# Planning the order of an attention and two-MLP kernel with a shared SBUF port, and folding in pairs

## The chip, the cores and the metric

The kernel runs on one core of a Trainium2 chip. The core's engines run side by side, each through its own list of instructions in order: TensorE (matmul, PE in the rows), VectorE (DVE), ScalarE (ACT), GpSimd (POOL), and SyncE (SP), which here issues most DMAs. An instruction that needs another engine's result waits on a semaphore, and everything behind it on its own engine waits too. SBUF is the on-chip memory, PSUM the matmul's accumulators (eight banks, `bank` in the rows). The metric is the device time of one execution in microseconds; the median of three runs of the kernel before is 742.17 us (740.36 to 742.63).

## The reference

```python
a = softmax(phi)                      # over the sequence, axis 2
k_m, v_m = a^T k, a^T v               # 32 memory rows for each of 4 x 8 heads
attn = softmax(q k_m^T / 8) v_m       # 4 x 8 heads, 576 tokens, 64 wide
x = attn, heads beside each other     # 2304 tokens x 512
x = ((x w_a) * (x w_b)) w_out         # 512 -> 1536 -> 512
h = x w_in                            # 512 -> 2048
out = (h * sigmoid(1.702 h)) w_out2   # 2048 -> 512
```

All in float32. The kernel splits each float32 operand into a high and a low part (fp32r) and multiplies in three passes, high x high, low x high, high x low.

## The kernel before, in words

**Stages on TensorE.** (1) Attention, to about 119 us, by eight steps `n` (batch `b`, half of the heads `g`): `memory(n)` transposes phi (L554 to L580), makes the memory keys and values (L596, L618) and the scores (L635), and `softmax` makes the attention weights `attn`, split in high and low. (2) The values are never multiplied with the weights: `fold(g, b)` (L798) multiplies the values of batch `b` into group `g` of w_a and w_b, 24 folds of 16 small fp32 matmuls, each followed by `fold_out`: a ScalarE copy (L818) and a VectorE subtraction (L820) for each of two banks, which make the high and low part of the folded weights `eff`. `gated` (L852) multiplies attn with a folded weight, 48 matmuls for a fold in two halves `u` (24 each), and multiplies the two products (L876). (3) `project` (L1014, to 373 us) is w_out by Strassen's seven products. (4) `step` and `quad` (L1290, to 547) are w_in, by seven products again, with the additions on VectorE (L1332, one input in PSUM) and the gate on ScalarE. (5) `proj2` (L1499) and `proj2_seven` (L1530) are w_out2.

**Combines.** Each split into high and low (`hi_lo`) is a ScalarE copy (L349) and a subtraction; Strassen's sums of weights and tokens are additions and subtractions of SBUF tiles; the softmax has two more. All go through `combine` (L343), which lets the planner choose GpSimd or VectorE. `sum_tokens` (L896) is always GpSimd's. `decode_piece` (L445, L449, L451) turns pieces of weights that come as 64-bit words into float32; L451 is VectorE's.

**What sets the order.** No list is written by hand. `Order` holds a clock for each engine and a set of streams (generators) with priorities. Each stream asks for an engine, with the time from which it can start and a duration; the planner starts the request that can start first (in steps of 40 ns), then by priority, and moves the engine's clock on. For a choice of engines (`_plan`) it takes the one that would end first, with a handicap in ns for VectorE (`W0` until the last stage, then `W1`). DMA landings are reckoned from a rate and a delay (`RATE0` in the first stage). The instructions come out in the order in which the planner starts them, and the chip keeps that order on each engine. The planner's numbers never reach the chip. While the first weights are not there, `warm_up` puts fill matmuls (L1605) on TensorE, as many as the planner's time asks for.

**Durations before.** `dve`, `act` and `pool` reckon fixed costs plus a rate; the class `Lengths` holds them and is switched between stages by `measured()`, `crowded()`, `calm` and `short()`. Where GpSimd or VectorE may combine, the durations are multiplied by `Lengths.pool` and `Lengths.both`.

Of the kernel before, what the change touches and what calls it, by code (L numbers as in the profile page):

```python
# [20 lines left out]
HOP, HOP_PE = 130.0, 200.0  # L21
W0 = 300.0
W1 = 0.0
# [12 lines left out]
PT1 = 15  # L36
FRONT = 1.0, 1.0, 1.0
RATE0 = 300.0, 2500.0
RATE = 330.0, 3000.0
# [6 lines left out]
PY = 5  # L46
RX = 12
BETWEEN = (0, 2, 4, 3, 3, 2, 2, 0)

# [6 lines left out]

class Lengths:
    dve, act, psum = 68, 94, 52
    six, wide, three = 740, 2.54, 650
    pool, both, slow = 1.0, 1.0, 1.0  # L60


def measured():
    Lengths.dve, Lengths.act, Lengths.psum = 150, 205, 160
    Lengths.six, Lengths.wide, Lengths.three = 795, 2.71, 690
    Lengths.pool, Lengths.both, Lengths.slow = 1.15, 1.4, 1.15


def crowded():
    measured()  # L70
    Lengths.pool, Lengths.both, Lengths.slow = 1.3, 1.75, 1.55


def short():
    Lengths.dve, Lengths.act, Lengths.psum = 68, 94, 52
    Lengths.pool, Lengths.both, Lengths.slow = 1.0, 1.0, 1.0


def dve(n, fast=False):
    return Lengths.dve + n / (1.92 if fast else 0.96)  # L80


def act(n, psum=False):
    return (Lengths.psum if psum else Lengths.act) + n / 1.2


def pool(n):
    return 150 + 2.1 * n
# [18 lines left out]
class Order:  # L107
# [9 lines left out]
    def __init__(self):  # L117
        self.clock = {PE: 0.0, ACT: 0.0, DVE: 0.0, POOL: 0.0}
        self.dma, self.marks, self.streams, self.count = 2000.0, {}, [], 0

        self.handicap = {DVE: W0}
        self.rate, self.land = RATE0

# [41 lines left out]
    def _plan(self, s):  # L165

        r = s[3]
        if not isinstance(r[0], dict):
            t = max(self.clock[r[0]], r[1] + (70.0 if r[0] == PE else 0.0))
            return (t if len(r) < 4 else max(t, min(x[1] for x in r[3].free))), r[0], r[2]  # L170
        best = None
        for e, d in r[0].items():
            t = max(self.clock[e], r[1])
            before = sum(
                x[3][2] for x in self.streams if x is not s and x[3][0] == e and x[:2] < s[:2] and x[3][1] <= t + d
            )
            if best is None or t + before + d + self.handicap.get(e, 0.0) < best[0]:
                best = t + before + d + self.handicap.get(e, 0.0), (t, e, d)
        return best[1]

    def run(self):
        while self.streams:
            if self._settle():
                continue
            plans = []
            for s in self.streams:
                r = s[3]
                if (isinstance(r[0], dict) or r[0] in self.clock) and (len(r) < 4 or r[3].free):
                    plans.append((self._plan(s), s))
            (t, e, d), s = min(plans, key=lambda x: (x[0][0] // 40, x[1][0], x[1][1]))  # L190
            self.clock[e] = t + d
            r = s[3]
            what = e if isinstance(r[0], dict) else r[3].take() if len(r) > 3 else None
            self._resume(s, (t + d + (HOP_PE if e == PE else HOP), what))
# [3 lines left out]
def tile_mem_attention_moe_moe2(  # L198
# [140 lines left out]
    def combine(t, dst, in0, in1, op, n):  # L339

        both = {POOL: Lengths.pool * pool(n), DVE: Lengths.both * dve(n)}
        t, e = yield {DVE: dve(n)} if alone[0] else both, t
        (nc.gpsimd if e == POOL else nc.vector).tensor_tensor(out=dst, in0=in0, in1=in1, op=op)  # L343
        return t
# [91 lines left out]
    def decode_piece(t, i, name, part, n, m):  # L436
# [5 lines left out]

        slow = Lengths.slow
        t, _ = yield ACT, t, act(512)
# [4 lines left out]
        nc.scalar.activation(out=lw, in_=top, func=AF.Copy, scale=2.0 ** -5, bias=2.0 ** -6 - 0.5)  # L449
        t, _ = yield DVE, t, slow * dve(512)  # L450
        nc.vector.scalar_tensor_tensor(  # L451
# [78 lines left out]
    def memory(n):  # L530
# [8 lines left out]
        if n >= NHG:  # L539

            t, e = yield {POOL: 900, ACT: act(HG * C0 * M)}, max(t, et[1])
            src = ph[0].rearrange("p h c m -> p c h m")
            dst = et[0].rearrange("p c s x -> p c (s x)").rearrange("p c (h m) -> p c h m", h=HG)
            if e == POOL:
                nc.gpsimd.tensor_copy(dst, src)
            else:
                nc.scalar.activation(out=dst, in_=src, func=AF.Copy)
        part = 240 if n < NHG else 70
        t, ba = yield PE, t, part * last, bank_a
# [23 lines left out]

        t, _ = yield PE, t, 70 * last
# [4 lines left out]
        t1, _ = yield PE, t2, 70  # L579
        nc.tensor.transpose(bb[0][:, P:2 * P], et[0][:, last].rearrange("p s x -> p (s x)"), ident)  # L580
# [140 lines left out]
    def close_attention():  # L721
# [15 lines left out]
        pa.release()  # L737
        measured()
        nonlocal py, pw
# [87 lines left out]
    def gated(g, b, u):  # L827
# [10 lines left out]
        for j, i in ((0, 0), (1, 0), (0, 1), (1, 1)) if wide else ((0, 0), (0, 1), (1, 0), (1, 1)):  # L838
            if True:
                if not wide:  # L840
                    t, ps = yield PE, t0, Lengths.six, bank_m
                    dst = ps[0]
                elif j == 0:
                    t, ps = yield PE, t0, Lengths.six, pair_s
                    dst = ps[0][:, j]
                else:
                    t, _ = yield PE, t0, Lengths.six
                    dst = ps[0][:, j]
# [43 lines left out]
    def sum_tokens(t, g, b, gr):  # L892
        b11, b21, b12, b22 = (gr[0][:, i] for i in range(4))
        for dst, in0, in1 in ((b11, b12, b11), (b12, b22, b12), (b22, b22, b11), (b21, b21, b22)):
            t, _ = yield POOL, t, Lengths.pool * pool(U)
            nc.gpsimd.tensor_tensor(out=dst, in0=in0, in1=in1, op=ALU.subtract)  # L896
# [8 lines left out]
    def have(*key):  # L905
        return od.marks.get(key)
# [241 lines left out]

    def calm():

        for p in (1, 2):
            for r in range(2):
                yield "mark", "yc", p, r
        measured()

    def room_projected():

        od.spawn(9, calm())
        nonlocal p2
# [16 lines left out]
    def room_last():  # L1176

        short()
        alone[0] = True
# [29 lines left out]
        for p in range(F2 // P // 2):  # L1209
            yield "mark", "wt", p  # L1210
        short()
        give(fw_s, views(acc, 2 * FN, 1))
# [394 lines left out]
    def main():  # L1607
        yield from all_gated()
        od.spawn(9, part_again())
        room_gated()  # L1610
        crowded()
        for p in range(NP):
# [23 lines left out]
    with tc.manual_schedule():  # L1636
# [7 lines left out]
        n0 = 2 * NHG  # L1644
        measured()
        Lengths.pool, Lengths.both, Lengths.slow = FRONT

# [54 lines left out]
```

## Time and profile before

| What | us |
|---|---|
| Median of three runs | 742.17 |
| The profiled execution | 740.76 |
| Its span, first to last instruction | 739.0 |
| TensorE busy | 729.0 (99%) |
| VectorE busy | 535.2 (72%) |
| ScalarE busy | 437.9 (59%) |
| GpSimd busy | 294.1 (40%) |

A busy share is an average over stages. The waits that end the kernel are found where TensorE stops; how full another engine is in that stretch says whether it can be the cause. An instruction's row gives its start and duration; on VectorE and GpSimd the duration holds what it waits for the other's use of SBUF.

### The profile page before, as it was taken

What the parts mean: (1) busy time and instruction counts of PE and PEld (TensorE: products, weight loads), DVE (VectorE), ACT (ScalarE), POOL (GpSimd) and SP (SyncE); (2) the same over time, 40 slices, a digit from 0 to 9 for tenths busy, and PEclk for the clock granted to TensorE, in tenths of its full rate; (3) what the DMA queues carried; (4) which work ended last, traced back from release to release, by engine and by line L of the source; (5) the groups of instructions that cost most, each with busy time, mean ns of one, the idle gap of its engine ahead of it and who ended that gap; (6) DMA issues with size and microseconds to landing.
All of it is one profiled execution on the core that took longest, in us unless ns stands there. A gap on an engine that the chain in (4) does not pass through costs nothing.

```text
span 739.0 us, 14874 instructions
## 1 busy us (share of the span) xinstructions
PE 729.0 (99%) x5480; PEld 687.0 (93%) x5480; DVE 535.2 (72%) x910; ACT 437.9 (59%) x852; POOL 294.1 (40%) x278
## 2 busy tenths in 40 slices
PE   9999999999999999999999999999999999999997
PEld 8877888888889999999999999999998889999997
DVE  3988786568983447945999666676657988888774
ACT  3877664677873447547867676666555564444441
POOL 0414376458896616824998343233250000000000
PEclk9999999999999999999999999999999999999999
DMA  8999854886688875676536888875597474444411
GB/s 269 333 342 298 293 200 153 260 282 218 227 257 281 283 203 165 177 207 190 200 114 203 278 251 267 269 258 186 190 298 244 158 233 137 125 144 144 143 30 29
DMA packets 112600, 157.74 MB, mean 213 GB/s; under 512 B 8592, under 2 KB 89232, under 8 KB 112528
## 3 DMA queue, kind: packets, MB, share of 16 engines
q1 hardware_dynamic: 107168, 147.32, 62.8%
q10 hardware_dynamic: 5360, 9.47, 3.7%
q8 instruction: 43, 0.70, 0.4%
q14 instruction: 29, 0.24, 0.1%
HBM read 104.20 MB, written 52.56 MB: 212 GB/s over the span
## 4 chain that ended last, share of the span: by engine, by line
PE 89%; DVE 4%; DMA 4%; issue 1%; ACT 1%; SPq 0%; POOLq 0%; ACTq 0%; POOL 0%; DVEq 0%
PE bank L1290 22%; PE bank L852 21%; PE bank L1530 19%; PE bank L1014 16%; PE bank L798 3%; DMA raw<-w2d 3%; PE bank L1605 2%; PE bank L596 1%; DMA acc<-g2d 1%; DVE attn L343 1%; PE bank L514 1%; DVE w L343 1%; DVE acc L343 1%; PE bank L635 1%; PE bank L576 0%
## 5 line engine op out<-in xcount | busy, mean ns | idle before, releaser
L852 PEld LDWEIGHTS bank<-attn,eff 128*128 128x128 f32 x1152 | 154.2, 188 | 15.4 <-issue 5.2
L852 PE MATMUL bank<-attn,eff 128*128 128x288 f32 x1152 | 162.8, 298 | 0.0
L349 ACT ACTIVATE w<-acc 128x512 fp32r<-128x512 f32 (+2 forms) x144 | 83.9, 591 | 76.9 <-PE bank L1530 47.8
L1332 DVE TENSOR_TENSOR acc<-bank,acc 128x384 f32<-128x384 f32 x168 | 89.4, 552 | 46.4 <-PE bank L1290 30.9
L343 DVE TENSOR_TENSOR w<-acc,w 128x512 fp32r<-128x512 f32 (+2 forms) x122 | 83.0, 685 | 26.3 <-ACT w L349 26.0
L349 ACT ACTIVATE attn<-acc 128x768 fp32r<-128x768 f32 (+2 forms) x84 | 62.6, 752 | 54.9 <-PE bank L1014 38.9
L1014 PE MATMUL bank<-attn,w 128*128 128x384 f32 x504 | 91.9, 335 | 0.7 <-DVE attn L343 0.7
L343 DVE TENSOR_TENSOR attn<-acc,attn 128x768 fp32r<-128x768 f32 (+2 forms) x61 | 67.1, 1111 | 31.9 <-ACT attn L349 30.7
L1014 PEld LDWEIGHTS bank<-attn,w 128*128 128x128 f32 x504 | 87.6, 188 | 2.0 <-DVE attn L343 1.4
L1342 ACT ACTIVATE acc<-acc 128x384 f32<-128x384 f32 x96 | 48.4, 522 | 26.5 <-DVE acc L1332 25.7
L343 DVE TENSOR_TENSOR acc<-acc 128x512 f32<-128x512 f32 (+2 forms) x90 | 60.8, 686 | 0.8 <-POOL w1b L343 0.5
L1290 PE MATMUL bank<-attn,w 128*128 128x384 f32 x288 | 55.1, 334 | 0.0
L896 POOL TENSOR_TENSOR gr<-gr 128x288 f32<-128x288 f32 x48 | 44.2, 922 | 18.7 <-DMA g1d<-gr 8.2
L343 POOL TENSOR_TENSOR attn<-acc,attn 128x768 fp32r<-128x768 f32 (+1 forms) x22 | 37.7, 1726 | 34.6 <-ACT attn L349 34.6
L343 POOL TENSOR_TENSOR w<-dm,w 128x256 fp32r<-128x256 f32 x35 | 30.8, 894 | 51.2 <-ACT w L349 51.1
L1530 PE MATMUL bank<-attn,w 128*128 128x256 f32 x336 | 50.0, 284 | 1.0 <-ACT w L349 0.7
L1290 PEld LDWEIGHTS bank<-attn,w 128*128 128x128 f32 x288 | 50.4, 188 | 0.0
L1014 PE MATMUL bank<-attn,w1b 128*128 128x384 f32 x252 | 47.6, 336 | 0.2 <-DVE attn L343 0.2
L1290 PE MATMUL bank<-w1b,w 128*128 128x384 f32 x224 | 46.2, 334 | 0.0
L1530 PEld LDWEIGHTS bank<-attn,w 128*128 128x128 f32 x336 | 44.5, 192 | 1.4 <-ACT w L349 1.0
L1014 PEld LDWEIGHTS bank<-attn,w1b 128*128 128x128 f32 x252 | 43.9, 188 | 0.9 <-DVE attn L343 0.5
L1290 PE MATMUL bank<-w 128*128 128x384 f32 x224 | 43.8, 334 | 0.0
(172 smaller groups left out, 1374.7 us busy)
## 6 DMA issues: line engine op xcount, KB each, us to landing
acc<-g1d SPq DMA_DIRECT2D x63, 384.0 KB, 3.7
g2d<-acc SPq DMA_DIRECT2D x96, 192.0 KB, 4.1
acc<-g2d SPq DMA_DIRECT2D x14, 1024.0 KB, 6.4
raw<-in_moe_w_out_dram SPq DMA_DIRECT2D x24, 512.0 KB, 4.9
raw<-in_moe_w_in_dram SPq DMA_DIRECT2D x16, 512.0 KB, 5.1
g1d<-gr SPq DMA_DIRECT2D x12, 576.0 KB, 5.3
g1d<-acc SPq DMA_DIRECT2D x8, 576.0 KB, 4.8
raw<-in_moe_w_a_dram SPq DMA_DIRECT2D x16, 256.0 KB, 4.2
```

The source lines that it names most:

```text
L343: (nc.gpsimd if e == POOL else nc.vector).tensor_tensor(out=dst, in0=in0, in1=in1, op=op)
L349: nc.scalar.activation(out=hi, in_=src, func=AF.Copy)
L514: nc.tensor.transpose(ps[0][:, i * P:(i + 1) * P], qs[0][:, 2 * (c0 + i):2 * (c0 + i) + 2, :].rearrange("p e d -> p (e d)"), ident,)
L798: nc.tensor.matmul(ps[c][0][row(h), :], bdv[b][half, h, :], wt["wab", g, h][0][half, :], start=True, stop=True)
L852: nc.tensor.matmul(dst[:, :U], e[:, c, sw, i * CW + j * P:i * CW + (j + 1) * P], attn(b, mv, c, u * U, U), start=(n == 0), stop=(n == 3 * ...
L896: nc.gpsimd.tensor_tensor(out=dst, in0=in0, in1=in1, op=ALU.subtract)
L1014: nc.tensor.matmul(ps[0][:, :N2], w1_of(a, g, sw)[:, r * P:(r + 1) * P], b[0][:, mv, i], start=(first and q == n == 0), stop=(q == NG1 // ...
L1290: nc.tensor.matmul(ps[0][:, :N2], w[:, sw, r, :], y[mv][r], start=(n == 0), stop=(n == 5))
L1332: nc.vector.tensor_tensor(out=s[0], in0=ps[0][:, :N2], in1=x[0], op=ALU.add)
L1342: nc.scalar.activation(out=c[0], in_=c[0], func=AF.Gelu_apprx_sigmoid)
L1530: nc.tensor.matmul(ps[name][0][:, :NB], x[0][:, sw, c, :], moving(b, h // 2 + c, mv), start=(h == c == n == 0), stop=(h > 0 and c == K4 - ...
L1605: nc.tensor.matmul(ps[0][:, :P], ident, ident, start=True, stop=True)
```

## The change

The planner's durations become one set for all stages: `dve(n)` 72 + n / 0.96, `act(n)` 100 + n / 1.2 (56 from PSUM). `Lengths` and its switches go. A combine's duration and some others are marked `Held`: a `Held` request on VectorE or GpSimd can start only when the previous `Held` one, on either engine, has ended (`self.port`). The handicap of VectorE goes from +300 to -300, so the planner takes VectorE unless GpSimd would end over 300 ns sooner. The reckoned rate of the first DMAs goes from 300 to 335 bytes a ns, their delay from 2500 to 1700. In `all_gated`, once attention is closed (`have("close")`), no fold is made while a folded weight is left, and then two are made one behind the other.

```diff
-W0 = 300.0
+W0 = -300.0
-RATE0 = 300.0, 2500.0
+RATE0 = 335.0, 1700.0
+SIX = 798.0
...
-class Lengths:
-    dve, act, psum = 68, 94, 52
-    six, wide, three = 740, 2.54, 650
-    pool, both, slow = 1.0, 1.0, 1.0
-def measured():
-    Lengths.dve, Lengths.act, Lengths.psum = 150, 205, 160
-    Lengths.six, Lengths.wide, Lengths.three = 795, 2.71, 690
-    Lengths.pool, Lengths.both, Lengths.slow = 1.15, 1.4, 1.15
-def crowded():
-    measured()
-    Lengths.pool, Lengths.both, Lengths.slow = 1.3, 1.75, 1.55
...
+class Held(float):
+    pass
...
-def dve(n, fast=False):
-    return Lengths.dve + n / (1.92 if fast else 0.96)
+def dve(n):
+    return 72 + n / 0.96
 def act(n, psum=False):
-    return (Lengths.psum if psum else Lengths.act) + n / 1.2
+    return (56 if psum else 100) + n / 1.2
...
         r = s[3]
         if not isinstance(r[0], dict):
-            t = max(self.clock[r[0]], r[1] + (70.0 if r[0] == PE else 0.0))
+            t = max(self.clock[r[0]], r[1] + (70.0 if r[0] == PE else 0.0), self.port if isinstance(r[2], Held) else 0.0)
...
         for e, d in r[0].items():
-            t = max(self.clock[e], r[1])
+            t = max(self.clock[e], r[1], self.port if isinstance(d, Held) else 0.0)
...
             self.clock[e] = t + d
+            if isinstance(d, Held):
+                self.port = t + d
...
-        both = {POOL: Lengths.pool * pool(n), DVE: Lengths.both * dve(n)}
+        both = {POOL: Held(pool(n)), DVE: Held(dve(n))}
...
-        t, _ = yield DVE, t, slow * dve(512)
+        t, _ = yield DVE, t, Held(dve(512))
...
-            t, e = yield {POOL: 900, ACT: act(HG * C0 * M)}, max(t, et[1])
+            t, e = yield {POOL: Held(700), ACT: act(HG * C0 * M)}, max(t, et[1])
...
-            t, _ = yield POOL, t, Lengths.pool * pool(U)
+            t, _ = yield POOL, t, Held(pool(U))
...
             if y:
                 folded.remove(y)
                 yield from gated(*y, 0)
-                x = ready_to_fold(True)
-            if x:
-                todo.remove(x)
-                folded.append(x)
-                yield from fold(*x)
+                x = None if have("close") and folded else ready_to_fold(True)
+            for _ in range(2):
+                if x:
+                    todo.remove(x)
+                    folded.append(x)
+                    yield from fold(*x)
+                x = ready_to_fold(True) if x and y and have("close") else None
```

The rest of the diff replaces `Lengths.six` by `SIX` and some reckoned transpose durations (70 by 110), and takes out the calls of the removed functions.

What comes out: TensorE, ScalarE and SyncE do the same work in another order (TensorE with 56 fill matmuls instead of 63). GpSimd has 148 instructions instead of 283, VectorE 1053 instead of 912: 135 combines move, and a few small PSUM copies go from ScalarE to VectorE. Lines of the changed kernel are 15 to 17 lower in these rows: L328 is L343, L435 is L451, L546 to L550 are L562 to L566, L644 to L660 are L660 to L676, L781 is L798, L803 is L820, L835 is L852, L859 is L876.

VectorE in the first attention steps, from the fourth decoded weight piece (L451, L435) to the first eff pair (L820, L803); sT is the score tile, sm and aT are the softmax's. Before:

```order
L451 SCALAR_TENSOR_TENSOR acc<-acc,raw_p_76 128x512
L667 TENSOR_SCALAR sm_116<-sm_116 128x9
L667 TENSOR_SCALAR sm_115<-sm_115 128x9
L660 TENSOR_REDUCE sm_117<-sT_112 128x9
L669 RECIPROCAL sm_116<-sm_116 128x9
L669 RECIPROCAL sm_115<-sm_115 128x9
L343 TENSOR_TENSOR sT_112<-sT_112,sm_116 128x288
L676 STREAM_TRANSPOSE aT<-sT_112 128x288
L820 TENSOR_TENSOR eff<-bank,eff 128x512 x2
```

Now:

```order
L435 SCALAR_TENSOR_TENSOR acc<-acc,raw_p_76 128x512
L651 TENSOR_SCALAR sm_116<-sm_116 128x9
L651 TENSOR_SCALAR sm_115<-sm_115 128x9
L644 TENSOR_REDUCE sm_117<-sT_112 128x9
L653 RECIPROCAL sm_116<-sm_116 128x9
L653 RECIPROCAL sm_115<-sm_115 128x9
L328 TENSOR_TENSOR sT_112<-sT_112,sm_117 128x288
L328 TENSOR_TENSOR sT_112<-sT_112,sm_116 128x288
L328 TENSOR_TENSOR sT_111<-sT_111,sm_115 128x288
L660 STREAM_TRANSPOSE aT<-sT_112 128x288
L803 TENSOR_TENSOR eff<-bank,eff 128x512 x2
```

Two sT combines that were GpSimd's stand ahead of the eff pair. On ScalarE the exponential of the second half of sT_112, which needs the first of the three, now stands ahead of the pair's copies (L818).

VectorE behind that pair, to the maximum for the next attention step (mx, L566 and L550). Before:

```order
L676 STREAM_TRANSPOSE aT<-sT_111 128x288
L665 TENSOR_REDUCE sm_117<-sT_112 128x9
L562 TENSOR_REDUCE mx_106<-bank 128x1
L667 TENSOR_SCALAR sm_117<-sm_117 128x9
L564 TENSOR_REDUCE mx_106<-bank 128x1
L669 RECIPROCAL sm_117<-sm_117 128x9
L566 TENSOR_SCALAR mx_106<-mx_106 128x1
```

Now:

```order
L328 TENSOR_TENSOR attn_83<-aT,attn_83 128x288
L660 STREAM_TRANSPOSE aT<-sT_111 128x288
L649 TENSOR_REDUCE sm_117<-sT_112 128x9
L546 TENSOR_REDUCE mx_106<-bank 128x1
L328 TENSOR_TENSOR attn_83<-aT,attn_83 128x288
L651 TENSOR_SCALAR sm_117<-sm_117 128x9
L548 TENSOR_REDUCE mx_106<-bank 128x1
L653 RECIPROCAL sm_117<-sm_117 128x9
L859 TENSOR_TENSOR gr<-bank,gr 128x288
L328 TENSOR_TENSOR sT_112<-sT_112,sm_117 128x288
L550 TENSOR_SCALAR mx_106<-mx_106 128x1
```

Three combines and a gated product (L859) stand ahead of the maximum now.

TensorE after attention, folds (L798, L781) and gated products (L852, L835). Before:

```order
L798 MATMUL bank<-acc,gr 32x512 x8
L852 MATMUL bank<-attn_84,eff 128x288 x48
L798 MATMUL bank<-acc,gr 32x512 x8
L852 MATMUL bank<-attn_84,eff 128x288 x24
L852 MATMUL bank<-attn_83,eff 128x288 x24
L798 MATMUL bank<-acc,gr 32x512 x8
```

Now:

```order
L781 MATMUL bank<-acc,gr 32x512 x16
L835 MATMUL bank<-attn_84,eff 128x288 x96
L781 MATMUL bank<-acc,gr 32x512 x16
L835 MATMUL bank<-attn_84,eff 128x288 x24
L835 MATMUL bank<-attn_83,eff 128x288 x72
L781 MATMUL bank<-acc,gr 32x512 x16
```

Seven pairs of folds stand like this after attention, and one during it; eight more folds during attention and after stay single. (The trace counts each of these fp32 matmuls as two instructions.)

## Rows read from the trace of the kernel before

**Rows 1.** The page's first part: busy us, share of the span, instructions.

```profile
PE 729.0 (99%) x5480; PEld 687.0 (93%) x5480; DVE 535.2 (72%) x910; ACT 437.9 (59%) x852; POOL 294.1 (40%) x278
```

**Rows 2.** Stretches of the span: busy us and instructions by engine, granted clock, DMA.

```profile
core 0: us, PE busy (x) PEld busy (x) DVE busy (x) ACT busy (x) POOL busy (x), PEclk, DMA share, GB/s
17.20:30.70 13.50, 13.50 (x161) 11.43 (x154) 13.08 (x34) 9.81 (x21) 4.40 (x6) 1.00 0.97 328
30.70:60.10 29.40, 26.91 (x312) 22.12 (x311) 25.88 (x58) 23.54 (x54) 8.81 (x11) 1.00 0.98 327
60.10:109.00 48.90, 48.90 (x575) 42.00 (x575) 37.37 (x86) 32.64 (x82) 23.37 (x25) 1.00 0.81 268
109.00:240.00 131.00, 131.00 (x1099) 115.04 (x1099) 90.61 (x124) 81.91 (x147) 92.89 (x86) 1.00 0.73 238
240.00:373.00 133.00, 132.05 (x754) 130.19 (x753) 88.31 (x85) 77.12 (x125) 77.87 (x58) 1.00 0.66 198
373.00:537.00 164.00, 164.00 (x948) 164.00 (x947) 119.45 (x209) 111.56 (x235) 75.49 (x84) 1.00 0.71 228
372.00:404.00 32.00, 32.00 (x187) 32.00 (x186) 30.95 (x46) 24.35 (x51) 31.51 (x27) 1.00 0.52 169
537.00:595.00 58.00, 57.03 (x271) 48.67 (x269) 43.13 (x99) 33.21 (x74) 10.59 (x8) 1.00 0.74 240
```

**Rows 3.** What TensorE waited for: us in total, times, longest.

```profile
PE bank L1014 <- DVE attn L343: 0.9, 3, 0.5
```

**Rows 4.** VectorE in order of time, 26 to 38 us: start, us, operation.

```profile
26.76 0.67 DVE L451 SCALAR_TENSOR_TENSOR acc<-acc,raw_p 128x512 uint32<-128x512 uint32 x1
...
28.10 0.91 DVE L343 TENSOR_TENSOR sT<-sT,sm 128x288 f32<-128x288 f32 x1
...
29.44 1.25 DVE L820 TENSOR_TENSOR eff<-bank,eff 128x512 fp32r<-128x512 f32 x2
...
32.63 0.21 DVE L566 TENSOR_SCALAR mx<-mx 128x1 f32<-128x1 f32 x1
```

**Rows 5.** ScalarE, TensorE and GpSimd in order of time, 28 to 36 us.

```profile
28.57 1.09 ACT L818 ACTIVATE eff<-bank 128x512 fp32r<-128x512 f32 x2 [1.98 <-PE bank L798]
...
30.77 3.41 PE L852 MATMUL bank<-attn,eff 128*128 128x288 f32 x24
...
34.45 0.60 PE L576 MATMUL bank<-ident,et 128*128 128x128 f32 x4
...
35.04 0.80 POOL L343 TENSOR_TENSOR attn<-aT,attn 128x288 fp32r<-128x288 f32 x1 [1.07 <-ACT attn L349]
```

**Rows 6.** VectorE and GpSimd by line and shape: count, busy, mean ns, idle.

```profile
L1332 DVE TENSOR_TENSOR acc<-bank,acc 128x384 f32<-128x384 f32 x168 | 89.4, 552 | 46.4 <-PE bank L1290 30.9 <-ACT w L349 6.2 <-ACT raw L449 3.2
...
L343 DVE TENSOR_TENSOR attn<-acc,attn 128x768 fp32r<-128x768 f32 x50 | 61.7, 1242 | 31.9 <-ACT attn L349 30.7 <-PE bank L1014 0.6
...
L343 DVE TENSOR_TENSOR acc<-acc 128x384 f32<-128x384 f32 x9 | 12.2, 1368 | 0.0
...
L876 DVE TENSOR_TENSOR gr<-bank,gr 128x288 f32<-128x288 f32 x22 | 10.0, 455 | 8.3 <-PE bank L852 7.8 <-ACT raw_p L449 0.3
...
L660 DVE TENSOR_REDUCE sm<-sT 128x18 f32<-128x576 f32 x6 | 4.5, 746 | 0.0
...
L343 POOL TENSOR_TENSOR acc<-acc 128x384 f32<-128x384 f32 x15 | 20.4, 1366 | 1.1 <-DVE acc L343 1.0
```

**Rows 7.** TensorE: timeline, chain of waits, and the fold by line.

```profile
115.36 1.09 PE L798 MATMUL bank<-acc,gr 64*32 64x512 f32 x16
...
122.93 1.09 PE L798 MATMUL bank<-acc,gr 64*32 64x512 f32 x16
...
223.59 16.11 PE bank L852 x120
...
239.70 54.14 PE bank L1014 x312
...
L798 PE MATMUL bank<-acc,gr 64*32 64x512 f32 x320 | 22.2, 599 | 0.0
```

More of the change, by code (lines that the diff above doesn't have):

```diff
@@ L36 @@
 PT1 = 15
-FRONT = 1.0, 1.0, 1.0
-RATE0 = 300.0, 2500.0
+RATE0 = 335.0, 1700.0
 RATE = 330.0, 3000.0
@@ L54 @@
 )
-class Lengths:
-    dve, act, psum = 68, 94, 52
-    six, wide, three = 740, 2.54, 650
-    pool, both, slow = 1.0, 1.0, 1.0
-def measured():
-    Lengths.dve, Lengths.act, Lengths.psum = 150, 205, 160
-    Lengths.six, Lengths.wide, Lengths.three = 795, 2.71, 690
-    Lengths.pool, Lengths.both, Lengths.slow = 1.15, 1.4, 1.15
-def crowded():
-    measured()
-    Lengths.pool, Lengths.both, Lengths.slow = 1.3, 1.75, 1.55
-def short():
-    Lengths.dve, Lengths.act, Lengths.psum = 68, 94, 52
-    Lengths.pool, Lengths.both, Lengths.slow = 1.0, 1.0, 1.0
-def dve(n, fast=False):
-    return Lengths.dve + n / (1.92 if fast else 0.96)
+class Held(float):
+    pass
+def dve(n):
+    return 72 + n / 0.96
 def act(n, psum=False):
-    return (Lengths.psum if psum else Lengths.act) + n / 1.2
+    return (56 if psum else 100) + n / 1.2
 def pool(n):
@@ L117, in __init__ @@
     def __init__(self):
-        self.clock = {PE: 0.0, ACT: 0.0, DVE: 0.0, POOL: 0.0}
-        self.dma, self.marks, self.streams, self.count = 2000.0, {}, [], 0
+        self.clock, self.port = {PE: 0.0, ACT: 0.0, DVE: 0.0, POOL: 0.0}, 0.0
+        self.dma, self.marks, self.streams, self.count = 2800.0, {}, [], 0
         self.handicap = {DVE: W0}
@@ L441, in decode_piece @@
         mu = mf.bitcast(U32)
-        slow = Lengths.slow
         t, _ = yield ACT, t, act(512)
@@ L547, in memory @@
                 nc.scalar.activation(out=dst, in_=src, func=AF.Copy)
-        part = 240 if n < NHG else 70
+        part = 240 if n < NHG else 110
         t, ba = yield PE, t, part * last, bank_a
@@ L572, in memory @@
         nc.scalar.activation(out=et[0][:, last, :, 0], in_=even, func=AF.Exp, bias=m[2], accum_out=m[4])
-        t, _ = yield PE, t, 70 * last
+        t, _ = yield PE, t, 110 * last
         for c in range(last):
@@ L578, in memory @@
             )
-        t1, _ = yield PE, t2, 70
+        t1, _ = yield PE, t2, 110
         nc.tensor.transpose(bb[0][:, P:2 * P], et[0][:, last].rearrange("p s x -> p (s x)"), ident)
@@ L737, in close_attention @@
         pa.release()
-        measured()
         nonlocal py, pw
@@ L840, in gated @@
                 if not wide:
-                    t, ps = yield PE, t0, Lengths.six, bank_m
+                    t, ps = yield PE, t0, SIX, bank_m
                     dst = ps[0]
                 elif j == 0:
-                    t, ps = yield PE, t0, Lengths.six, pair_s
+                    t, ps = yield PE, t0, SIX, pair_s
                     dst = ps[0][:, j]
                 else:
-                    t, _ = yield PE, t0, Lengths.six
+                    t, _ = yield PE, t0, SIX
                     dst = ps[0][:, j]
@@ L1147, in room_kept @@
         give(f_s, views(acc, FN, 3, 2 * AN))
[L1149 to L1154, printed above, removed]
     def room_projected():
-        od.spawn(9, calm())
         nonlocal p2
@@ L1176, in room_last @@
     def room_last():
-        short()
         alone[0] = True
@@ L1210, in room_last @@
             yield "mark", "wt", p
-        short()
         give(fw_s, views(acc, 2 * FN, 1))
@@ L1610, in main @@
         room_gated()
-        crowded()
         for p in range(NP):
@@ L1644, in tile_mem_attention_moe_moe2 @@
         n0 = 2 * NHG
-        measured()
-        Lengths.pool, Lengths.both, Lengths.slow = FRONT
         def loads():
```

## The prediction

> **What bounds the kernel now.** I read the page's busy times first, then the stretches, then TensorE's waits, then the rows around those waits. TensorE is busy 729.0 of 739.0 us [rows 1], so at most 10 us can be gained by removing waits; more only by making TensorE's own work shorter. The stretches say where the waits lie: 2.49 us in 30.7:60.1, 0.95 in 240:373, 0.97 in 537:595, the rest at the two ends of the span; from 60.1 to 240 and from 373 to 537 TensorE never stops [rows 2]. The granted clock is 1.00 in every stretch [rows 2], so no term for the clock is needed. In the projection all of TensorE's waits are on VectorE's attn writes, 0.9 us in three [rows 3].
>
> VectorE is the second engine to watch: 535.2 us in all [rows 1], but 13.08 of 13.50 in 17.2:30.7 and 25.88 of 29.40 in 30.7:60.1 [rows 2]. Before 60 us the kernel is bound by VectorE nearly as much as by TensorE.
>
> The price of sharing is in the grouped rows. A 384-wide tensor_tensor from SBUF takes 1368 ns on VectorE and 1366 on GpSimd when both run at once; the same width with one input in PSUM takes 552 on VectorE [rows 6]. So side by side each pays for the other, and a VectorE operation that reads PSUM does not. A 768-wide one has a mean of 1242; alone I put it at 0.95 us, the 552 and 384 more columns at the slope between 288 wide (455) and 384 wide (552), 1.0 ns [rows 6].
>
> **The change part by part.** Terms are against the profiled execution: span 739.0, 1.76 around it, 740.76. The median shown, 742.17, is 1.41 above that.
>
> *1. Combines go from GpSimd to VectorE.* The order has 135 fewer tensor_tensors on GpSimd and as many more on VectorE. What that costs depends on the stretch.
>
> (a) Up to the first gated product. VectorE has no room here, and the order puts three 288-wide sT combines between the fourth decoded weight piece (L451, whose row ends at 27.43 [rows 4]) and the first eff pair (L820), where there was one. Alone a 288-wide one takes 0.455 [rows 6]: three take 1.37 against the 0.91 of the one beside GpSimd [rows 4], +0.5. ScalarE's first eff copy (L818) also stands behind an exponential now that needs the first of the three; it started at 28.57 [rows 5] and I reckon with 29.8. The eff pair ended at 30.69 [rows 4]; I expect 31.7, and the first gated matmul, at 30.77 now [rows 5], near 31.8: +1.0, between +0.5 (the three combines alone) and +1.6. The seven fewer fill matmuls change nothing: the fold behind them waits for that fourth decode.
>
> (b) From there to the fourth eff pair, at 60.1. The next attention step hangs on L566, whose row ends 2.15 us after the eff pair [rows 4]; the order puts four more 288-wide operations between, 4 x 0.455 less their overlap, +1.6. So L566 ends near 35.4 instead of 32.84, and the transposes that need its exponential (34.45 [rows 5]) come near 37, with TensorE standing for 1.5. The attn low part that the next six gated matmuls need was made by GpSimd, ending at 35.84 [rows 5]; now it is VectorE's, behind this queue, near 38.4. By 39 us TensorE is thus 2.5 to 3 late. It catches up in part, since it was waiting for VectorE here before too. In this stretch VectorE gets four 288-wide (0.455) and three 576-wide combines (0.75, as its 576-wide reduction [rows 6]), 4.1 us, and 0.5 of small copies: 25.9 + 4.6 = 30.5 us of work where 29.4 held 3.5 idle. If all that idle is used, the shift of the fourth eff pair is +1.0 and 1.1; if none, +1.0 and 4.6. TensorE has 0.8 us of transposes ahead of its wait for these pairs that came behind it before. So (a) and (b) together lie between +1.3 and +4.8, less what the freed port gives back, which I put at up to 1.0, since most of VectorE's operations here read PSUM. I take +2.2, near the lower end: an engine that was already 88% busy with work waiting will use its idle.
>
> (c) 60 to 109 us. Six 576-wide combines come, 4.5 us, into the 11.5 that VectorE is idle. Their cover is gated matmuls, queued ahead on a TensorE without waits. +0.4, between 0 (there is no wait to give back) and +1.5.
>
> (d) 240 to 373. The waits fall where both engines combine tokens and a 768-wide split is slowed. GpSimd is nearly empty there now. A split is needed every 2.08 us (12 of the 312 matmuls in 54.14 us [rows 7]) and brings 0.95 for itself and about two 384-wide combines, 1.1: 2.05, just covered, with splits held ahead. -0.9; 0 if VectorE's queue takes the place of the wait.
>
> (e) 373 to 537. VectorE has 119.45 and GpSimd 75.49 of 164 [rows 2]. Some 57 operations move, about 26 us; some 7 of slowing goes. VectorE gets to 139 of 164, still not the bound: 0.
>
> (f) From 537 the orders hardly differ: 0, with the 0.97 of waits as the bound to either side.
>
> *2. Folds two at a time.* One fold (16 instructions of L798) and 48 gated matmuls have a period of 122.93 - 115.36 = 7.57 us; 120 gated matmuls in one run take 16.11, so 48 take 6.44. A lone fold costs 1.13 [rows 7]. Its run lasts 1.09 and one of its instructions 0.60, so its second eight start 0.46 to 0.49 after the first eight [rows 7]: a fold that follows a fold adds 0.92 to 0.98 and saves 0.15 to 0.21. The order has seven such pairs after attention and one during it: 8 x 0.18 = -1.4, between -0.6 (half is lost to waits for banks) and -1.7. This is TensorE's own work in a stretch without waits, so it comes off the end directly. The new wait, four eff subtractions in a row on VectorE (2.7 us), is covered: the first of the pair is needed a fold and 24 gated matmuls (3.2 us) later.
>
> Sum: 2.2 + 0.4 - 0.9 - 1.4 = +0.3. 740.76 + 0.3 = 741.1 in the profile's terms, and 1.4 more in the median's: **742.5**. With the bounds of the largest terms (+0.3 - 0.9 - 1.7 and +4.8 + 0.4 - 0.9 - 0.6) this case lies between 739.9 and 745.9.
>
> **A page against the trace.** The Trainium skill, page "SBUF — State Buffer", section "SBUF: two separate sides", says that VectorE and GpSimd hold a shared port pair in turns, for whole instructions, and only where VectorE has two SBUF inputs. The 1368 against 552 ns agrees. It speaks against the change as well: beside VectorE's additions from PSUM, GpSimd's work would be free. By it stage (e) would lose what GpSimd did beside them, as in rival C.
>
> **Rivals.**
> *B, slower: attention queues on VectorE.* The 1.5 us that TensorE stands for the third head group's L566 comes again for each of the five groups after it: 7.5, of which 1.6 is in the forecast. For it: VectorE is 97% and 88% busy there. Against: it is 24% idle from 60 us, with gated work ahead of TensorE. It decides once VectorE passes some nine tenths in 60:109. 742.5 + 5.9 = 748.4.
> *C, slower: VectorE binds the first quads.* In 372:404 VectorE and GpSimd are both full, 30.95 and 31.51 of 32 [rows 2], making token operands for the quad that starts near 404. The order leaves GpSimd eight 384-wide operations; some nineteen go over, at 0.55, 10.5 us, and ten slowed ones give back 0.8 each [rows 6]: 2.5 us late, for which TensorE stands. Against: a combine on VectorE alone takes less than half as long as two side by side. It decides if the last operand comes after the third quad's end. 745.0.
> *D, faster: the front costs nothing.* VectorE, no longer slowed, keeps step; +2.2 and +0.4 go, and half of the 2.49 us of waits in 30.7:60.1 too. For it: the slowed rows. Against: the order puts the added operations ahead of those that TensorE waits for. 742.5 - 2.6 - 1.2 = 738.7.
> That the change does not do what it says is excluded: the order shows both parts.
>
> **How the numbers follow.** Forecast 0.46, B 0.13, C 0.11, D 0.30. A measurement of this kernel tells about 0.3%, 2.2 us, from no change: 739.9 to 744.4 is the same. D is faster, B and C are slower, and of the forecast's own range a tail of 0.03 is: 0.30, 0.43, 0.27. The range for eight in ten takes in D with the other half of the 2.49 us gone too (737.5) and the lower half of B: 737.5 to 747.0; the likeliest case alone has 739.9 to 745.9.
>
> **What would show it.** Right: the first gated matmul at 31.4 to 32.3 us; TensorE's waits from there to 62 us at 4 to 6 us in sum; fold pairs that lengthen the period by about 2.1; no waits near 294, 300 and 366. Wrong: waits of TensorE for VectorE between 60 and 109 (B) or 388 and 405 (C); a gated start no later than 30.8 (D); waits of over 0.2 us behind the fold pairs, which would take part 2 back.

## The result, and the profile after

The changed kernel takes 745.06 us (741.35 to 748.70, ten runs), the kernel before beside it 740.43 (739.27 to 742.63, ten): a ratio of 1.0053, interval 1.0030 to 1.0076. It is slower by half a per cent, where "the same" was forecast with 742.5 us; the time lies in the range of 737.5 to 747.0.

The page's first part and four stretches of the profiled execution after (745.58 us, span 743.8) answer to [rows 1, 2]:

```profile
PE 729.0 (98%) x5466; PEld 688.4 (93%) x5466; DVE 564.4 (76%) x1051; ACT 430.5 (58%) x842; POOL 135.6 (18%) x143
```

```profile
17.20:30.70 13.50, 13.48 (x164) 10.84 (x149) 13.01 (x38) 8.73 (x18) 2.02 (x3) 1.00 1.02 350
30.70:60.10 29.40, 27.11 (x304) 21.03 (x302) 27.84 (x67) 22.57 (x51) 4.23 (x5) 1.00 0.95 312
60.10:109.00 48.90, 47.86 (x561) 40.14 (x562) 44.54 (x96) 33.60 (x83) 16.54 (x20) 1.00 0.80 271
...
375.00:539.00 164.00, 164.00 (x948) 164.00 (x947) 130.83 (x264) 108.31 (x236) 25.72 (x27) 1.00 0.68 226
```

GpSimd's work fell from 294.1 to 135.6 us, VectorE's rose from 535.2 by 29 only. What GpSimd gave up cost VectorE a fifth of it. TensorE's busy time is the same by chance: matmuls at half clock count longer (below), while the fill matmuls take 16.5 us instead of 18.7 and the folds take less. Three long waits are new (the list of waits, answering to [rows 3]: us in total, times, longest):

```profile
PE bank L560 <- ACT et L552: 2.8, 2, 2.2
PE bank L1505 <- ACT w L334: 2.0, 1, 2.0
PE bank L999 <- ACT attn L334: 1.6, 1, 1.6
```

The three lie near 59, 595 and 254.5 us. None of them is a wait for VectorE. The stage table, from the start of the first matmul of each line:

| Stage | before | after | difference |
|---|---|---|---|
| to the end of the gated stage | 239.54 | 239.79 | +0.25 |
| projection (L1014, now L999) | 133.72 | 135.69 | +1.97 |
| quads and first part of w_out2 | 218.43 | 218.28 | -0.15 |
| rest, to the end of the span | 147.31 | 150.04 | +2.73 |

So the profiled execution loses its 4.8 us in two places where no loss was forecast. (0.4 of the last 2.73 lies behind TensorE's last matmul, where the outputs are stored.) The projection's loss, on TensorE in order of time, then by stretches:

```profile
252.28 2.25 PE L999 MATMUL bank<-attn,w 128*128 128x384 f32 x12
256.15 0.62 PE L999 MATMUL bank<-attn,w 128*128 128x384 f32 x2 [1.63 <-ACT attn L334]
257.14 1.37 PE L999 MATMUL bank<-attn,w 128*128 128x384 f32 x4 [0.37 <-DVE attn L328]
```

```profile
240.00:255.00 15.00, 14.52 (x84) 14.20 (x82) 5.45 (x5) 3.90 (x6) 8.42 (x8) 1.00 0.82 274
255.00:257.50 2.50, 0.98 (x4) 0.66 (x5) 1.37 (x3) 2.50 (x4) 0.00 (x0) 1.00 0.03 10
257.50:260.50 3.00, 3.00 (x11) 3.00 (x10) 2.25 (x4) 0.41 (x2) 0.00 (x0) 0.50 0.62 154
260.50:373.00 112.50, 112.27 (x646) 111.91 (x646) 78.83 (x120) 69.32 (x115) 1.23 (x1) 1.00 0.67 195
...
595.00:598.70 3.70, 1.50 (x10) 1.09 (x9) 1.21 (x2) 1.87 (x4) 0.00 (x0) 1.00 0.51 155
598.70:602.00 3.30, 3.30 (x18) 3.30 (x17) 3.23 (x7) 2.17 (x5) 0.00 (x0) 0.52 0.67 173
```

TensorE stands for 2.00 us in two pieces, and behind the wait the granted clock (the share of its full speed that TensorE is given) is 0.50, 1.2 instead of 2.4 GHz, for 3.4 us; then it is back at 1.00. The matmuls start 0.32 us apart there instead of 0.173: ten of them, 1.5 us lost on top of the wait. The same happens at 595. So the low clock costs some 3 of this execution's 4.8 us.

The ten runs point the same way: the one with a mean clock of 1.000 took 741.35 us, the two with 0.992 took 747.01 and 748.70, and a line through all ten gives 0.80 us for each 0.001 and 741.05 at 1.000. By that line 3.7 of the 4.6 us go with the clock, and 0.6 would be left at full clock (0.9 in the one run that had it). That is rather an upper estimate of the clock's share. The mean also holds a low clock behind TensorE's last matmul, which costs nothing (1.6 us in the profiled execution, from 742.2 us on), and longer waits, which bring the clock down, cost time themselves.

What the wait at 254.5 was for, ScalarE, then GpSimd and SyncE, in order of time:

```profile
248.14 0.85 ACT L334 ACTIVATE attn<-acc 128x768 fp32r<-128x768 f32 x1 [1.23 <-PE bank L999]
248.89 0.47 ACT L1021 ACTIVATE gr<-bank 128x384 f32<-128x384 f32 x1
254.87 0.49 ACT L1021 ACTIVATE gr<-bank 128x384 f32<-128x384 f32 x1 [5.51 <-issue]
255.26 2.30 ACT L334 ACTIVATE attn<-acc 128x768 fp32r<-128x768 f32 x3
```

```profile
245.24 5.40 POOL L879 TENSOR_TENSOR gr<-gr 128x288 f32<-128x288 f32 x4
...
250.67 0.36 SPq L880 DMA_DIRECT2D g1d<-gr  x1
```

ScalarE stands 5.5 us before its second product copy (L1021), though the product had long been in its bank. The copy writes part of the `gr` buffer in which GpSimd makes its last sums (L879) until 250.64; SyncE stores them from 250.67 (the last row above), landing at 254.80, and the copy starts at 254.87. Three token splits that TensorE needs stand behind it. In the kernel before the last sums lay in the other buffer, `acc`, and both copies ran at 248.66:

```profile
248.66 0.85 ACT L1036 ACTIVATE gr<-bank 128x384 f32<-128x384 f32 x2
245.75 5.54 POOL L896 TENSOR_TENSOR acc<-acc 128x288 f32<-128x288 f32 x5 [1.44 <-DVE attn L343]
```

ScalarE's order is the same in both kernels here; what differs is in which buffer the last sums happen to lie.

### The profile page after: what moved, and what is told of

Its sections match the earlier page's. It is cut to its first block, busy times and chain, and to the rows that moved or that the text cites. A ratio compares the mean times of both kernels' runs of the same rounds, so it can differ in the third digit from the quotient of the medians.

```text
span 743.8 us, 14793 instructions
## 1 busy us (share of the span) xinstructions
PE 729.0 (98%) x5466; PEld 688.4 (93%) x5466; DVE 564.4 (76%) x1051; ACT 430.5 (58%) x842; POOL 135.6 (18%) x143
## 4 chain that ended last, share of the span: by engine, by line
PE 86%; DMA 5%; DVE 4%; issue 1%; ACT 1%; POOL 1%; SPq 0%; ACTq 0%; DVEq 0%; POOLq 0%
PE bank L1265 23%; PE bank L835 20%; PE bank L1505 19%; PE bank L999 16%; PE bank L781 3%; PE bank L1474 2%; DMA acc<-g2d 1%; DMA q<-in_q_dram 1%; PE bank L580 1%; DVE w L328 1%; DMA kv<-in_k_dram 1%; DMA g1d<-acc 1%; DMA raw_p<-in_moe_w_b_dram 1%; DMA raw<-in_moe_w_b_dram 1%; POOL gr L879 1%
## 5 line engine op out<-in xcount | busy, mean ns | idle before, releaser
L835 PEld LDWEIGHTS bank<-attn,eff 128*128 128x128 f32 x1152 | 154.2, 188 | 11.3 <-issue 3.5
L835 PE MATMUL bank<-attn,eff 128*128 128x288 f32 x1152 | 163.3, 298 | 0.4 <-DVE eff L803 0.4
L328 DVE TENSOR_TENSOR w<-acc,w 128x512 fp32r<-128x512 f32 (+2 forms) x135 | 87.9, 657 | 28.6 <-ACT w L334 27.8
L328 DVE TENSOR_TENSOR attn<-acc,attn 128x768 fp32r<-128x768 f32 (+2 forms) x75 | 66.0, 893 | 49.1 <-ACT attn L334 48.2
L999 PE MATMUL bank<-attn,w 128*128 128x384 f32 x504 | 92.7, 338 | 2.2 <-ACT attn L334 1.6
L999 PEld LDWEIGHTS bank<-attn,w 128*128 128x128 f32 x504 | 88.5, 190 | 3.2 <-ACT attn L334 1.9
L334 ACT ACTIVATE attn<-acc 128x768 fp32r<-128x768 f32 (+2 forms) x80 | 60.9, 768 | 49.3 <-PE bank L999 40.3
L328 DVE TENSOR_TENSOR acc<-acc 128x512 f32<-128x512 f32 (+2 forms) x101 | 61.4, 628 | 0.1
L879 POOL TENSOR_TENSOR gr<-gr 128x288 f32<-128x288 f32 x52 | 51.2, 989 | 49.4 <-DMA g1d<-gr 21.3
L1505 PE MATMUL bank<-attn,w 128*128 128x256 f32 x336 | 50.1, 284 | 2.2 <-ACT w L334 2.0
L999 PE MATMUL bank<-attn,w1b 128*128 128x384 f32 x252 | 47.4, 336 | 0.0
L1505 PEld LDWEIGHTS bank<-attn,w 128*128 128x128 f32 x336 | 44.7, 193 | 2.6 <-ACT w L334 2.2
L999 PEld LDWEIGHTS bank<-attn,w1b 128*128 128x128 f32 x252 | 44.5, 190 | 0.0
L1505 PE MATMUL bank<-w 128*128 128x256 f32 x294 | 41.0, 283 | 0.0
L1265 PEld LDWEIGHTS bank<-w1b,w 128*128 128x128 f32 x224 | 39.5, 188 | 0.0
```

Source lines behind the costliest of these rows:

```text
L334: nc.scalar.activation(out=hi, in_=src, func=AF.Copy)
L835: nc.tensor.matmul(dst[:, :U], e[:, c, sw, i * CW + j * P:i * CW + (j + 1) * P], attn(b, mv, c, u * U, U), start=(n == 0), stop=(n == 3 * ...
L999: nc.tensor.matmul(ps[0][:, :N2], w1_of(a, g, sw)[:, r * P:(r + 1) * P], b[0][:, mv, i], start=(first and q == n == 0), stop=(q == NG1 // ...
L1265: nc.tensor.matmul(ps[0][:, :N2], w[:, sw, r, :], y[mv][r], start=(n == 0), stop=(n == 5))
L1505: nc.tensor.matmul(ps[name][0][:, :NB], x[0][:, sw, c, :], moving(b, h // 2 + c, mv), start=(h == c == n == 0), stop=(h > 0 and c == K4 - ...
```

## The experiments

Theory T: the loss is a wait behind that buffer and the clock that falls behind it and behind the wait near 595, while the front loses because combines on VectorE stand ahead of what TensorE waits for. Rivals: R, the fold pairs make the last products late; V, VectorE binds the projection now; W, the waits themselves cost, the clock little.

**Folds one at a time again** (e1, the second half of the diff undone).

```
-                x = None if have("close") and folded else ready_to_fold(True)
-            for _ in range(2):
...
+                x = ready_to_fold(True)
+            if x:
```

> The changed kernel with folds one at a time again; the planner's part alone. Both kernels were read before: the changed one stands 2.0 us near 254.5 us because ScalarE's second product copy writes a buffer whose last sums GpSimd is still storing, and TensorE's clock halves for 3 us behind that wait and behind one near 595.5. Theory T (buffer and clock): the last sums lie in the same buffer here, so the wait near 254 and the slow stretch stay, the folds cost 0.35 us more for each of seven pairs: about 747.5 us. Rival R (pairs): the fold pairs make the last gated products late; without them the wait near 254 goes, and only the folds' 2.4 us come back: about 744.

747.24 us, ratio 1.0077 (1.0052 to 1.0102). T's number comes, but only in part by T's way. The wait in the projection stays, shorter (1.1 and 0.4 us, at 262.7), and the fold period is 7.57 us again; but in the profiled execution the clock stays at 1.00 behind it, and behind 1.43 us at the late place, and falls behind the wait near 59 (2.16 us) instead. R falls: taking the pairs away gains nothing, and the wait does not go.

**Pairs alone on the kernel before** (e2).

> The kernel before with the fold pairs alone; the old planner. T: the pairs save 0.35 us each (a period of 14.79 against twice 7.57), seven or so of them, 2.1 to 2.5 us off the end of the gated stage; the last sums lie in the other buffer, so no wait near 254 and a granted clock of 1.00: about 738.2 us, ratio 0.997. R: a wait of 1.5 to 2 us near 254 with a slow clock behind it: about 741.5 us, ratio 1.001. The prediction's price of a pair (0.18) would give 739.2.

743.72 us, ratio 1.0044 (1.0030 to 1.0058): neither, T by 5 us. A pair has its period of 14.80 where it runs freely, and the wait near 254 is absent, as T wanted; but under the old planner two pairs wait for their eff subtractions, and the projection waits more (list of waits; the profiled execution also began 2.4 us late, at an unchanged order):

```profile
PE bank L1016 <- DVE attn L343: 1.8, 3, 0.8
PE bank L852 <- DVE eff L820: 1.7, 3, 0.9
PE bank L1016 <- POOL attn L343: 1.4, 2, 1.1
```

Of the 1.7, 1.24 stand behind the pairs, near 197 and 213. The pairs' own saving is there; of it the profiled execution keeps 0.4 us by the end of the gated stage, and its projection is 2.4 us longer than before, so more is given back than was saved.

**Other buffers for the copies** (e3). No engine's order changes by a row.

```
-        give(hc_s, views(p2_m, N2, 7))
+        give(hc_s, [views(p2_m, N2, 7)[i] for i in (0, 5, 6, 4, 3, 2, 1)])
```

> The changed kernel with the seven buffers of the projection's copies handed out in another order (0, 5, 6, 4, 3, 2, 1); every engine's order stays word for word, so only what the second copy has to wait for changes. T: the wait near 254 (1.6 and 0.4 us) and the 3 us at half clock behind it go, 1.3 to 2.0 for the wait and 1.5 for the clock: about 742 us, ratio to the kernel before 1.001 to 1.003. Rival V (VectorE is what binds the projection now that it has the combines): TensorE waits as long, for VectorE's splits: 745 us as before.

743.79 us, ratio 1.0036 (1.0018 to 1.0054). The wait is gone; ScalarE and the stretch:

```profile
250.00 0.85 ACT L334 ACTIVATE attn<-acc 128x768 fp32r<-128x768 f32 x1 [1.23 <-PE bank L999]
250.75 0.85 ACT L1021 ACTIVATE gr<-bank 128x384 f32<-128x384 f32 x2
252.08 0.85 ACT L334 ACTIVATE attn<-acc 128x768 fp32r<-128x768 f32 x1 [0.48 <-PE bank L999]
```

```profile
240.00:373.00 133.00, 132.77 (x770) 132.48 (x769) 92.39 (x138) 78.78 (x128) 10.42 (x11) 1.00 0.69 205
```

The projection takes 131.5 us, 4.2 less than in the changed kernel and 2.2 less than before; V falls, and the projection's loss is the buffer's. The gain in the median is smaller, 1.3 us, and the two ratios' intervals overlap. One reason seen is that here the clock fell behind the wait near 59, which it had not in the changed kernel's profiled execution (both fell at the late place):

```profile
58.80:61.20 2.40, 0.17 (x2) 0.09 (x2) 2.40 (x5) 2.40 (x6) 2.15 (x3) 0.95 0.97 275
61.20:64.50 3.30, 3.30 (x16) 3.30 (x17) 2.21 (x5) 1.41 (x5) 0.00 (x0) 0.52 0.97 321
```

A line through its eleven runs gives 738.0 us at a clock of 1.000, an estimate: no run had that.

**VectorE's handicap at +300 again** (e4, `W0 = 300.0` in the changed kernel).

> The changed kernel with VectorE's handicap at +300 ns again instead of -300: GpSimd gets 198 instructions instead of 148, the shared-port model and the fold pairs stay. T: the last sums still lie in the buffer that the second copy writes, and GpSimd is no less busy: the wait near 254 stays and both slow stretches; 744 to 746 us. V: with combines back on GpSimd the waits for VectorE's work shrink: about 742 us.

751.47 us, ratio 1.0137 (1.0111 to 1.0162): both wrong. The wait in the projection stays (1.1 and 0.4, at 260) and leaves the clock at 1.00; the front is 5.6 us later than in the changed kernel, and a wait of 0.75 and 1.37 us appears in the quads near 467, with the clock at half behind it.

**Filling matmuls in the waits** (e5 on the changed kernel; e6 on e3's, without the second place). The third edit, near 595, is like the second.

```
+        for _ in range(6 * (n == 4)):
+            nc.tensor.matmul(bb[0][:, 3 * P:], ident, ident, start=True, stop=True)
...
+                    for _ in range(20 * (p == r == 0 and name == "P5" and q == 1)):
+                        x = w1_of(a, 0, HI)
+                        nc.tensor.matmul(ps[0][:, N2:], x[:, :P], x[:, P:], start=False, stop=False, skip_group_check=True)
```

> The changed kernel with matmuls into unused PSUM columns put at the three places where TensorE stands about 2 us (near 59, 254.5 and 595.5 us): 6 of 128 columns in float32, 20 of 128 and 12 of 256 in one pass, some 1.3 us each, ahead of the matmul that waits. They lie in the wait, and nothing else is moved. T (waits of 2 us bring the clock down, and that is most of the loss): the granted clock is 1.00 in nearly every run and the time 741 to 742 us, as the changed kernel's runs without a slow clock have it. Rival W (the loss is the waits themselves, the clock costs little): 745 us or more, since the waits are still there.

> The changed kernel with the other order of the copies' buffers (which took the wait near 254 away) and with the filling matmuls near 59 and 595.5 us. T: no slow clock, and without the wait near 254 about 738.5 us, ratio to the kernel before 0.997 to 0.998. W: 743 to 744 us, as with the buffers alone.

746.44 (ratio 1.0071, 1.0046 to 1.0095) and 745.83 (1.0070, 1.0055 to 1.0084): T's 741 to 742 and 738.5 did not come, and e5's number is W's. The filling near 59 spoils the test, since it was made to wait, too, for an exponential that reads the same PSUM bank:

```profile
63.26 1.01 PE L560 MATMUL bank<-ident 128*128 128x128 f32 x3 [2.94 <-ACT et L556]
```

The 2.15 us became 2.94, the filling came behind it, and the clock fell all the same, in e6 for 6.8 us instead of 3.4. At that clock the twelve instructions of the filling took 2.7 us, to 65.98 (the row ends with the stretch asked for). The gated stage ended at 246.1 and 247.3 us, where the same order without this filling ends at 239.8 to 242.1 (changed kernel, e3, e10); some 1 us of it is there already at the first gated matmul (31.55 and 31.52 against 30.21 to 30.67), ahead of the filling. At the two late places the clock stays at 1.00; stretches of e5, from the projection's start to its end and from the place of the wait near 595:

```profile
246.00:380.00 134.00, 133.77 (x780) 133.48 (x779) 91.89 (x139) 77.89 (x127) 9.59 (x10) 1.00 0.67 198
599.40:605.00 5.60, 5.38 (x42) 5.14 (x43) 3.90 (x7) 4.05 (x8) 0.00 (x0) 1.00 0.77 231
```

**Filling at the two late places alone** (e10, the first two added lines left out).

> The changed kernel with the filling matmuls near 254.5 and 595.5 us alone; those near 59 us are left out, since there they had to wait for the same exponential themselves and stood behind it. The projection should take 133.8 us instead of 135.7, and the stage from 593.8 us on 144.3 instead of 145.7 at most. T: about 742 us, and a granted clock under 1.00 only by the wait near 59 (then 743.5). W (the clock costs little): 745 us.

743.48 us, ratio 1.0033 (1.0019 to 1.0047), 1.6 below the changed kernel. The profiled execution's projection takes 133.79 us; while TensorE works the clock is 1.00 but behind the wait near 59. The four runs with a mean clock of 0.999 took 741.6 to 743.8, the five from 0.996 to 0.998 743.2 to 744.9; six of the changed kernel's ten lay at 0.992 to 0.995. T's second number (743.5) comes, though the interval of one ratio reaches into the other's, so W is not excluded. Nor is it shown that the filling held the clock: in e5 and e10 the load behind the late wait landed 7.9 and 7.8 us after its issue instead of 9.1, so that some 0.8 us would have been left to wait there (an estimate from the load's landing), and ScalarE's copy at 254.5 stood 4.3 and 4.9 us instead of 5.5. In e1 waits of 1.1 + 0.4 and of 1.43 us left the clock at 1.00 with no filling.

**A hybrid** (e7): the planner of before until attention is over, then the changed planner's durations, shared port and handicap, and the pairs. The main lines, in the kernel before:

```
+def settle():
+    measured()
+    Lengths.dve, Lengths.act, Lengths.psum, Lengths.six = 72, 100, 56, 798
+    Lengths.pool, Lengths.both, Lengths.slow, Lengths.late = 1.0, 1.0, 1.0, True
...
         pa.release()
-        measured()
+        settle()
+        od.handicap[DVE] = -300.0
```

> The planner of before up to the end of attention, the changed planner (shared port, handicap -300, new durations) and the fold pairs from there on. Up to 109 us the order is that of before. T (the front's 2.4 us come from the combines on VectorE ahead of what TensorE waits for): the front costs nothing, the pairs give 2.2 to 2.5, no wait of 2 us near 59, and the projection as with the changed planner: 738 to 739.5 us; up to 2 more if a wait near 254 or 595 brings the clock down. Rival F (the front's loss is the DMA model or chance, not the combines' place): 741 us or more with the front as late as in the changed kernel.

738.24 us (736.15 to 741.19, twelve runs), ratio 0.9967 (0.9955 to 0.9979): faster than both kernels. Its front is that of before, first gated matmul at 30.77 us and as many gated products by 117.8; the projection:

```profile
240.00:371.00 131.00, 130.77 (x755) 130.48 (x754) 91.47 (x137) 78.02 (x127) 10.12 (x9) 1.00 0.70 206
```

131.5 us instead of 133.7. The changed planner is thus worth 2 us there, once its front and its unlucky buffer are left away. In the profiled execution the clock never falls while TensorE works.

**What in the front costs** (e8: the hybrid with `W0 = -300.0` from the start; e9: the hybrid with `RATE0 = 335.0, 1700.0`).

> The hybrid (planner of before up to the end of attention, changed planner and fold pairs after it), with VectorE's handicap at -300 ns from the start: in attention 21 of 30 softmax combines on VectorE where the hybrid has 14 and the changed kernel 28; reckoned durations and DMA rate in attention as before. T (the combines' place on VectorE makes the front late): gated products behind at 117.8 us by 10 to 18, end of the gated stage 1 to 2.4 us later than the hybrid's 239.7, 739.5 to 740.5 us. F (the reckoned DMA rate or the other durations make it late): as the hybrid, 738.2 us.

> The hybrid with the changed kernel's reckoned rate and delay of the first DMAs (335 bytes a ns, 1700 ns) and nothing else: 11 of 30 softmax combines on VectorE. T: no later than the hybrid, 738.2 us. F: 2 us and more later than the hybrid, 740.5 us, with waits of TensorE for the first loads or behind them.

744.40 (ratio 1.0046, 1.0033 to 1.0059) and 746.07 (1.0076, 1.0063 to 1.0088). Each theory has the sign right in its run and misses the size by some 4 to 6 us: the handicap alone costs 6.2 us against the hybrid (4.0 of it by the end of the gated stage in the profiled executions), the DMA rate and delay alone 7.8 (5.0), though they leave fewer combines on VectorE. But e9 is not the changed kernel's reckoning of the DMAs. The change also moves the time at which the planner's DMA clock starts (`self.dma`) from 2000 to 2800 ns, so that with the delay of 1700 the fixed part of a first load's reckoned landing stays as before (2800 + 1700 = 2000 + 2500); e9 leaves the 2000, and reckons the first loads 0.8 us sooner than the changed kernel does. What the changed reckoning does by itself was not run. The changed kernel's front has the handicap and the full reckoning and costs 2.4 (below). So the front's loss can't be put down to the combines' place; any of the edits makes another order there, and each order tried (also e4's) was later than that of the kernel before. What it is in each stays open.

**The hybrid with folds one at a time** (e11).

> The hybrid (planner of before up to the end of attention, changed planner from there on) with folds one at a time: the pairs' part alone is taken from it. T: fold periods of 7.57 us again instead of 14.79 for two, so seven pairs' 2.4 us come back, less the waits behind pairs that the hybrid shows (0.88 and 0.15 us): end of the gated stage near 241, 739.5 to 740.2 us. Rival P (pairs give nothing once the waits behind them are paid): 738.2 us as the hybrid.

738.88 us (737.38 to 739.77), ratio 0.9967 (0.9955 to 0.9979), the hybrid's: P. From the first gated matmul to the end of the gated stage both take 208.7 to 208.8 us. Pairs save 0.35 us each, but the hybrid's pairs wait 0.88 and 0.15 us for the copies of gated products, and three of their periods are 15.1 to 15.2 us instead of 14.8. Nothing measurable is left.

## Why the prediction was right or wrong

- **The number.** That the time lies in the range is in part luck. Against the kernel before, the forecast was +0.3 us and the runs say +4.6. The 742.5 stood on a median of three, 742.17, which ten runs put at 740.43; and the range reached up to 747.0 to let in half of rival B, which did not come. Terms (d) and (f) fell outside their own bounds.
- **The clock.** "The granted clock is 1.00 in every stretch, so no term for the clock is needed": this step failed. The low clock cost some 3 of the 4.8 us in the profiled execution, and at most 3.7 of the 4.6 by the line through the runs. The reading was right for the profile before, whose longest wait inside a stage is 1.18 us. The change brought waits of 2.0 to 2.2, and each can cost another 1.5 us.
- **(a), first gated matmul.** Forecast 31.8, measured 30.67. The three combines took 1.48 us (1.37 forecast) and the eff pair ended 0.46 later, but the first gated matmul needs only the pair's first half.
- **(b) and (c), the front.** L566, now L550, ended at 34.50 (35.4 forecast, 32.84 before). At 117.8 us the changed kernel had made 352 gated matmuls where the kernel before had made 370, with as many folds: 18 x 0.134 = 2.4 us behind, against 2.2 + 0.4 forecast. TensorE's waits from 30.7 to 62 us came to 3.3, under the 4 to 6 forecast. The sum was right, its parts were not: (a) gave nothing, TensorE's first standstill was 0.66 us instead of 1.5, and the 2.15 us near 59 had no term of its own. That the loss comes from VectorE's queue is not shown (e8, e9, e4): that longest wait is for an exponential of ScalarE that stands behind two eff copies.
- **(d), the projection.** -0.9 forecast, +1.97 measured. The splits went as reckoned: 969 ns for a 768-wide one (0.95 forecast), the waits near 294, 300 and 366 gone. The wait that took their place was not VectorE's queue, but a buffer that GpSimd had filled late and SyncE still stored from. Without it (e3, e7) the term is -2.2, more than the 0.95 of waits in the list: the starts of the matmuls before show 2.45 us over the usual 0.173, of which 1.65 around the three waits, since each also stretches the interval behind it by 0.11 and hides some 0.16, and 0.8 in stretched intervals that the list leaves out.
- **(e).** Right: VectorE got to 130.83 of 164 us (139 forecast), and TensorE never waits. By the Trainium skill's page cited in the prediction, "SBUF — State Buffer", section "SBUF: two separate sides", GpSimd's work beside VectorE's additions from PSUM would have been free. The "only" in that citation is too strong, since the section also has VectorE take the shared pair in its 2-port modes. In this trace giving the work up cost nothing either.
- **(f), from 537 on.** "0": it cost 2.7. The load that the wait near 592 to 595 hangs on was issued as late as before, measured from TensorE's place (6.0 us ahead of L1505's first matmul, 5.9 before), but landed 9.1 us after its issue instead of 8.1. The wait grew from 1.2 us in three pieces to 2.2, and the clock fell. The profiled executions of other kernels with the same order here had 9.0 us (e3), 7.9 (e5) and 7.8 (e10), so chance has a share in the 1.0 us; the rest isn't settled, and no run took this wait away by itself.
- **Folds.** -1.4 forecast, -2.15 from 117.8 us to the end of the gated stage (2.4 behind at 117.8, 0.25 at the end). It is not a saving to count on: in the hybrid the waits behind the pairs take all of it back (e11). A pair's period:

```profile
147.76 1.95 PE L781 MATMUL bank<-acc,gr 64*32 64x512 f32 x32
149.64 12.98 PE L835 MATMUL bank<-attn,eff 128*128 128x288 f32 x96
162.55 1.95 PE L781 MATMUL bank<-acc,gr 64*32 64x512 f32 x32
```

14.79 us against 2 x 7.57: 0.35 saved, not 0.18, since two folds side by side also break the gated run once instead of twice. The forecast had priced the fold alone.
- **The rivals.** B and C did not come: TensorE has no wait from 62 to 109 us and none in 372 to 404. D is wrong for this kernel, though its sign came (a gated start at 30.67, no later than 30.8): the start did not tell whether the front would cost anything. A rival that a wait grows until the clock falls was missing, and it was the one that happened.

## What to carry to other kernels

Where TensorE is 99% busy, an edit of the order is to be judged by the longest wait that it can make as well as by the sum of waits: the listed 2.0 us in the projection cost 4.2 (e3). A planner that hands out buffers hides dependencies that the order of the instructions does not show; look for an engine that stands with its input long ready, and ask who still reads its output's place. Try a planner's new rules stage by stage: here they were worth 2 us in the projection and cost as much in attention, and the hybrid that has them in the later stages alone beat both kernels.

## What was not expected of the hardware

- The clock fell behind waits of 1.98 and 2.00 us, and in one kernel (e4) behind two of 0.75 and 1.37 close together; two of 1.1 and 0.4 left it at 1.00 (e1, e4). The same wait of 2.15 to 2.23 us near 59 left it at 1.00 in one profiled execution (the changed kernel's) and halved it in others (e1, e3, e10). It stayed at half for 3.4 us each time, in e6 for 6.8, while TensorE worked on.
- A list of waits understates them: 0.95 us in three waits listed in the projection before, 1.65 lost between starts of matmuls around them, 2.45 in the whole stage.
- A matmul into unused columns of a PSUM bank waited for ScalarE's read of other columns of that bank (e5, 2.94 us). The wait is on a semaphore that the program sets; whether the bank itself would have asked for it no run shows.
